# One level of Strassen's algorithm in the second stage of six batches of a fused attention and bilinear kernel

## The chip, the cores and the metric

The kernel runs on one core of one Trainium2 chip. TensorE (PE, with its weight loads shown as PEld), VectorE (DVE), ScalarE (ACT) and GpSimd (POOL) each run their own queue of instructions; SyncE (SP) issues most of the DMAs, and ScalarE's queue issues the stores of the output. The metric is the device time of one execution in microseconds (us): the median of 3 runs. A profile is one further execution; its span runs from the first to the last instruction.

## What is computed

```python
# x: (8, 8, 512, 64) = B, H, S, D     state: (8, 8, 32, 64)
scores  = x @ state^T / sqrt(D);   a  = softmax(scores);   xread = a @ state
scores2 = state @ x^T / sqrt(D);   a2 = softmax(scores2);  sread = a2 @ x
y = concat(xread, sread) over the token axis, heads side by side   # 4608 tokens x 512
h = ((y @ w1) * (y @ w2)) @ w3        # w1, w2: 512 x 1024, w3: 1024 x 1024
out = h @ w_out                       # w_out: 1024 x 512
```

There are 8 batches of 512 token rows (`xread`), and the 32 state rows of each batch (`sread`), which are worked off together at the end, 256 rows in all.

## The kernel before

**What is folded.** `w3 @ w_out` is computed once, into `wo` (1024 x 512), so that the bilinear part needs one product after the elementwise one. `w1` and `w2` are multiplied with each batch's `state` (`sw_steps`, L263, and `per_head`, L140), so that **stage 1** (`stage1`, L297) multiplies `at`, the transposed attention weights (256 values per token: 8 heads of 32 states), by `sw` and gets the two factors directly. Every operand of the large products is split into a high part (ACT casts it to float32r, L96) and a low part (DVE subtracts, L97), by `split` (L93), and a product of two such operands is three matmuls: hi with lo, hi with hi, lo with hi.

**One batch.** The hidden width 1024 is cut into 8 tiles `ft` of 128. For each `ft`, stage 1 runs 12 matmuls of 512 columns (2 factors, 2 tiles of the contraction, 3 parts) into a pair of PSUM banks, `two_banks` (3 such pairs turn). `hidden` (L287) evacuates it, with high priority: ACT copies one factor (L290), DVE multiplies it by the other (L291), ACT and DVE split the result into `g_hi` and `g_lo` (L96, L97), 128 x 512 each. **Stage 2** (`stage2`, L320, with `project`, L313) then takes the 4 token tiles `tt` one after the other: 8 `ft` times 3 matmuls, weights 128 x 128 of `g`, moving operand 128 x 512 of `wo`, all 24 into one bank (`bank`, 2 of these turn), which ACT copies out (L329) and stores from its own queue (L331).

**What runs beside it.** After the first token tile of stage 2 of batch b, `batch_stage2` (L360) runs the steps of `side_steps` (L335): two of the four `sw` units of batch b+1 (16 matmuls of 64 x 32 weights each, then a split of 128 x 1024), the scores of batch b+1 (`scores`, L178, 16 matmuls), the read of batch b (`read_state`, L233, 64 small matmuls with `a2_t` as weights), the other two `sw` units, and the rest of the softmax on DVE and ACT: transposes, maxima, exponentials, sums, and the split into `at_hi` and `at_lo` (L186 to L222). The transposed `e2` is moved block by block with DMAs on SP's queue into `a2_t` (`move_blocks`, L166; L225 to L231), and the read's result into `sread` (L254). At the end of stage 2 come the loads of x (`load_tokens`, `load_x`).

**What sets the order.** PE's and SP's instructions run in the order in which the program lists them (L64). Those of DVE and ACT are put in order when the kernel is built: of what can run, what the program lists first goes first, and what stands under `tc.high_priority()` ahead of the rest. Every engine then works its list strictly from the front. Batch 0 (L462 to L488) has its own, interleaved order and is not changed; batch 1 is the first in the plain loop (L520). The last part, `state_rows` (L492), waits for the last splits of batch 7 (`last_split`, L525), multiplies the 256 state rows with splits of `w1` and `w2` (`grp_z`, L504; L507 and L508) and runs stage 2 on them.

**Buffers that matter here.** `tmp` (4 of 128 x 512) serves the factor copies, and the output tiles; `g_hi` and `g_lo` have 8 buffers each; `work` 2; `x_d` and `x_s` 1 each.

Of the kernel before, what the change touches and what calls it, by code (L numbers as in the profile page):

```python
# [22 lines left out]
F32 = mybir.dt.float32  # L23
# [10 lines left out]
LAST = 5  # L34
PARTS = {0: (640, 1024), 1: (512, 1024)}
WARM = 15

@with_exitstack
def attn_bilinear_kernel(
# [134 lines left out]
    def attention_steps(b):  # L174
        xd = x_tiles[b]
        a2 = {}

        def scores():  # L178

            ps = two_banks()  # L180
            per_head(ps, b, lambda rows, j: xd[rows, j])
            yield
            flat = lambda t: t.rearrange("p k s -> p (k s)")

            s1 = work_tile()
# [37 lines left out]
            yield  # L223

            blocks = work_tile()  # L225
            with tc.issue_after(last[1].ins):
                nc.vector.transpose(out=flat(blocks), in_=flat(e2))
            a2["t"] = work_tile() if b < 2 else late.tile([P, KT, S], F32, name="a2_t")
            tiles = lambda t: t.rearrange("p k (t m) -> p (k t) m", m=P)
            move_blocks(lambda its, j: tiles(a2["t"])[its, :, j * NS:(j + 1) * NS],  # L230
                        lambda mine, c: tiles(blocks)[mine, :, c * NS:(c + 1) * NS])  # L231

        def read_state():  # L233

            xs = token_tiles[b]

            ps = (bank() if b else two_banks()[:, 0])[:, :KT * D].rearrange("p (k d) -> p k d", k=KT)
            for kt in range(KT):
                for t in range(NT):
                    for j in range(NP):  # L240
                        mine = slice(j * NS, (j + 1) * NS)
                        nc.tensor.matmul(  # L242
                            ps[mine, kt], a2["t"][:, kt, t * P + j * NS:t * P + (j + 1) * NS],
                            xs[:, t, 2 * j + kt], start=(t == 0), stop=(t == NT - 1),
                        )
# [45 lines left out]
            nc.vector.tensor_tensor(out=a_sb[:, :n], in0=a_sb[:, :n], in1=ps[:, 1, :n], op=ALU.mult)  # L291
            last_split[:] = split(g_hi, g_lo, a_sb[:, :n])

    def new_g():
        return [main.tile([P, NF], F32R, name=f"g_{part}", bufs=FT) for part in ("hi", "lo")]

    def stage1(b, ft, gs):  # L297
        half, c = divmod(ft * P, NF)
        ps = two_banks()
        hi, lo = at_tiles[b]  # L300
        for i in range(2):
            w_hi, w_lo = sw_tiles[b][half, i]
            k = 0
            for kt in range(KT):
                for w, a in ((w_hi, lo), (w_hi, hi), (w_lo, hi)):
                    nc.tensor.matmul(  # L306
                        ps[:, i], w[:, kt, c:c + P], a[:, kt], start=(k == 0), stop=(k == 3 * KT - 1)
                    )
                    k += 1
        gs.append(new_g())  # L310
        hidden(ps, S, *gs[-1])

    def project(ps, gs, tt, ft):  # L313
# [21 lines left out]
    def side_steps(b):  # L335


        if b == B:
            return [[reads[b - 1]], [], [], []]
        scores, reads[b], a2 = attention_steps(b)  # L340
        w = sw_steps(b)
        softmax = scores()
        first = partial(islice, softmax, 3)
        if b == 1:
            def rest():

# [6 lines left out]
        return [[w[0], w[1], product, reads[b - 1], w[2], w[3], lambda: softmax], [], [], []]  # L353

    def run(steps):
        for step in steps:
# [14 lines left out]
    with tc.tile_pool(name="pro", bufs=2) as pro:  # L371
# [115 lines left out]
        load_tokens(1)  # L487
        load_x(2)  # L488
    late = ctx.enter_context(tc.tile_pool(name="late", bufs=1))


    def state_rows():  # L492
        n = B * NS

        sr = late.tile([P, NP, 2, n], F32R, name="grp_sr")
        split(sr[:, :, 1], sr[:, :, 0], sread)
        gs = []
        for ft in range(FT):
            quarter, c = divmod(ft * P, NQ)
            ps = two_banks()  # L500
            for i in range(2):
                wh, wl = (late.tile([P, NP * P], F32R, name=f"grp_z{q}", bufs=3) for q in range(2))
                as_w = lambda t: t.rearrange("p (j f) -> p j f", j=NP)
                split(as_w(wh), as_w(wl), w_sb[:, quarter, i, :, c:c + P])  # L504
                for kt in range(NP):
                    ks = slice(kt * P, (kt + 1) * P)
                    nc.tensor.matmul(ps[:, i], wh[:, ks], sr[:, kt], start=(kt == 0), stop=False)  # L507
                    nc.tensor.matmul(ps[:, i, :n], wl[:, ks], sr[:, kt, 1], start=False, stop=(kt == NP - 1))  # L508
            gs.append([g[:, :n] for g in new_g()])
            sums = main.tile([P, 2, n], F32, name="tmp", bufs=4)  # L510
            halves = ps.rearrange("p i (half n) -> p i half n", n=n)
            nc.scalar.copy(out=sums, in_=halves[:, :, 1])
            nc.vector.tensor_tensor(out=sums, in0=sums, in1=halves[:, :, 0], op=ALU.add)
            nc.vector.tensor_tensor(out=sums[:, 0], in0=sums[:, 0], in1=sums[:, 1], op=ALU.mult)
            split(*gs[-1], sums[:, 0])
        for tt in range(n // P):
            stage2(gs, tt, [(out[tt * PER + q, S:], q * NS, NS) for q in range(PER)])


    for b in range(1, B):  # L520
        gs = []
        for ft in range(FT):
            stage1(b, ft, gs)
        batch_stage2(b, gs)
    with tc.issue_after(last_split[0].ins), tc.issue_after(last_split[1].ins):  # L525
        state_rows()

# [43 lines left out]
```

## Time and profile before

| | |
|---|---|
| median of 3 runs | 501.19 us (500.25 to 501.69) |
| span of the profiled execution | 498.4 us, at a granted TensorE clock of 0.999 |
| what lies around the span | 1.9 to 3.3 us, if the profiled execution took as long as one of the three runs |
| PE, PEld, DVE, ACT busy | 492.3, 362.8, 285.7, 219.3 us |
| HBM read, written | 38.27 MB, 8.91 MB |

Matmuls are pipelined, so the recorded time of one (about 390 ns for 512 columns) is longer than the distance between two; the distance is read from a chain or a timeline. Weight loads have records of their own (188 ns for 128 x 128), which overlap matmuls. From batch 1 on, the chain of waits repeats the same six pieces of PE work in every batch, some 49 us from one batch to the next; these are shown below.

### The profile page before, as it was taken

Reading aid. Unit: us, or ns where it says so; the run is one execution under the profiler, and the core shown is the slowest. Engines: PE = TensorE matmul, PEld = TensorE weight load, DVE = VectorE, ACT = ScalarE, POOL = GpSimd, SP = SyncE. Lnnn points to the kernel's source line nnn. Section 1 sums busy time; section 2 is a strip of 40 time slices with the busy share of each in tenths; the row PEclk is TensorE's granted clock in tenths of the full one; section 3 lists DMA queues with packets and bytes.
Section 4 is the critical chain, followed back from the end, with each engine's and each line's share of the span. In section 5 each row is a group of like instructions: output and inputs, shape, how many; then the busy total and the mean of one; then the engine's idle time right before and its main releaser. Section 6 shows DMA issues by size and latency. Waiting matters only on the chain.

```text
span 498.4 us, 7562 instructions
## 1 busy us (share of the span) xinstructions
PE 492.3 (99%) x3054; PEld 362.8 (73%) x3054; DVE 285.7 (57%) x394; ACT 219.3 (44%) x325; POOL 0.2 (0%) x4
## 2 busy tenths in 40 slices
PE   8999999999999999999999999999999999999996
PEld 6444467767867886788678867886788678888885
DVE  5669896772539343934393539354934493530780
ACT  4777884443444244334333434243424342431650
POOL 0000000000000000000000000000000000000000
PEclk9999999999999999999999999999999999999999
DMA  8996962013400350035003500350035003301001
GB/s 343 364 380 237 364 264 33 11 47 80 181 22 19 79 189 23 20 79 188 21 27 76 185 22 27 77 184 22 26 78 183 22 26 78 93 24 49 21 1 42
DMA packets 52323, 52.41 MB, mean 105 GB/s; under 512 B 42304, under 2 KB 43328, under 8 KB 47680
## 3 DMA queue, kind: packets, MB, share of 16 engines
q1 hardware_dynamic: 47488, 43.27, 26.3%
q10 hardware_dynamic: 4800, 8.65, 4.6%
q8 instruction: 24, 0.39, 0.3%
q14 instruction: 11, 0.09, 0.1%
HBM read 38.27 MB, written 8.91 MB: 95 GB/s over the span
## 4 chain that ended last, share of the span: by engine, by line
PE 95%; DVE 2%; ACT 2%; DMA 1%; issue 0%; DVEq 0%
PE ps_o L316 38%; PE ps L306 35%; PE ps L146 7%; PE ps L507 3%; PE ps_o L402 3%; PE ps_o L389 3%; PE ps L389 3%; PE ps L508 2%; PE ps_o L242 1%; DMA raw<-in_w_k_dram 1%; ACT ulps L125 0%; ACT w_sb L117 0%; ACT wo_hi L96 0%; DVE w L133 0%; DVE work L204 0%; DVE wo_lo L97 0%
## 5 line engine op out<-in xcount | busy, mean ns | idle before, releaser
L316 PE MATMUL ps_o<-wo_lo,g_hi 128*128 128x512 f32 x272 | 107.0, 394 | 0.0
L316 PE MATMUL ps_o<-wo_hi,g_hi 128*128 128x512 f32 x272 | 106.0, 390 | 0.0
L316 PE MATMUL ps_o<-wo_hi,g_lo 128*128 128x512 f32 x272 | 105.9, 389 | 0.0
L306 PE MATMUL ps<-at_lo,sw_hi 128*128 128x512 f32 x256 | 100.1, 391 | 0.0
L306 PE MATMUL ps<-at_hi,sw_lo 128*128 128x512 f32 x256 | 99.6, 389 | 0.0
L306 PE MATMUL ps<-at_hi,sw_hi 128*128 128x512 f32 x256 | 99.6, 389 | 0.0
L291 DVE TENSOR_TENSOR tmp<-tmp,ps 128x512 f32<-128x512 f32 x64 | 43.9, 687 | 77.0 <-ACT tmp L290 76.9
L97 DVE TENSOR_TENSOR g_lo<-tmp,g_hi 128x512 fp32r<-128x512 f32 (+1 forms) x72 | 47.5, 661 | 41.7 <-ACT g_hi L96 41.6
L96 ACT CAST g_hi<-tmp 128x512 fp32r<-128x512 f32 (+1 forms) x72 | 43.1, 599 | 53.6 <-DVE tmp L291 48.8
L290 ACT COPY tmp<-ps 128x512 f32<-128x512 f32 x64 | 37.7, 589 | 62.8 <-PE ps L306 52.2
L316 PEld LDWEIGHTS ps_o<-wo_lo,g_hi 128*128 128x128 f32 x272 | 51.0, 188 | 18.0 <-issue 7.5
L316 PEld LDWEIGHTS ps_o<-wo_hi,g_lo 128*128 128x128 f32 x272 | 51.1, 188 | 10.8
L316 PEld LDWEIGHTS ps_o<-wo_hi,g_hi 128*128 128x128 f32 x272 | 51.1, 188 | 10.3
L97 DVE TENSOR_TENSOR sw_lo<-ps,sw_hi 128x1024 fp32r<-128x1024 f32 (+1 forms) x34 | 38.4, 1155 | 32.8 <-ACT sw_hi L96 32.8
L306 PEld LDWEIGHTS ps<-at_lo,sw_hi 128*128 128x128 f32 x256 | 48.1, 188 | 10.9 <-issue 1.1
L306 PEld LDWEIGHTS ps<-at_hi,sw_hi 128*128 128x128 f32 x256 | 48.1, 188 | 10.2 <-issue 0.2
L306 PEld LDWEIGHTS ps<-at_hi,sw_lo 128*128 128x128 f32 x256 | 48.1, 188 | 10.0
L329 ACT COPY tmp<-ps_o 128x512 f32<-128x512 f32 x34 | 19.8, 583 | 76.1 <-PE ps_o L316 76.1
L96 ACT CAST sw_hi<-ps 128x1024 fp32r<-128x1024 f32 (+1 forms) x34 | 31.7, 967 | 14.3 <-PE ps L146 14.2
L146 PE MATMUL ps<-w_sb,st 64*32 64x512 f32 (+1 forms) x544 | 31.6, 572 | 0.0
L402 PE MATMUL ps_o<-w_sb,w 128*128 128x512 f32 x64 | 28.5, 599 | 0.1
L402 PEld LDWEIGHTS ps_o<-w_sb,w 128*128 128x128 f32 x64 | 11.8, 190 | 15.9 <-issue 13.8
(65 smaller groups left out, 417.9 us busy)
## 6 DMA issues: line engine op xcount, KB each, us to landing
raw<-in_w_k_dram SPq DMA_DIRECT2D x8, 1024.0 KB, 6.6
x_d<-in_x_d_dram SPq DMA_DIRECT2D x8, 1024.0 KB, 7.1
raw<-in_w_dram SPq DMA_DIRECT2D x8, 1024.0 KB, 6.3
x_s<-in_x_s_dram SPq DMA_DIRECT2D x8, 1024.0 KB, 5.4
out_dram<-tmp ACTq DMA_DIRECT2D x32, 256.0 KB, 2.0
raw<-in_w3t_dram SPq DMA_DIRECT2D x4, 1024.0 KB, 7.2
a_t<-work SPq DMA_DIRECT2D x96, 32.0 KB, 1.9
sread<-turned SPq DMA_DIRECT2D x128, 4.0 KB, 1.7
```

The lines of the kernel that those rows point to most:

```text
L96: nc.scalar.copy(out=hi, in_=src),
L97: nc.vector.tensor_tensor(out=lo, in0=src, in1=hi.bitcast(F32), op=ALU.subtract),
L146: nc.tensor.matmul(ps[j * NS:(j + 1) * NS, q], sts[b][rows, j], moving(rows, j), start=True, stop=True)
L290: nc.scalar.copy(out=a_sb[:, :n], in_=ps[:, 0, :n])
L291: nc.vector.tensor_tensor(out=a_sb[:, :n], in0=a_sb[:, :n], in1=ps[:, 1, :n], op=ALU.mult)
L306: nc.tensor.matmul(ps[:, i], w[:, kt, c:c + P], a[:, kt], start=(k == 0), stop=(k == 3 * KT - 1))
L316: nc.tensor.matmul(ps[:, :DO], g, wo[w][:, ft, :], start=(ft == 0 and k == 0), stop=(ft == FT - 1 and k == 2))
L329: stored[:] = [nc.scalar.copy(out=o, in_=ps[:, :DO])]
L389: nc.tensor.matmul(w34_ps[i][:, :DO], chunks[k][:, DO + i * P:DO + (i + 1) * P], w_out[k], start=(k == 0), stop=(k == FT - 1),)
L402: nc.tensor.matmul(w34_ps[i][:, :DO], w3s[i][:, k * P:(k + 1) * P], w_out[k], start=(k == 0), stop=(k == FT - 1))
L507: nc.tensor.matmul(ps[:, i], wh[:, ks], sr[:, kt], start=(kt == 0), stop=False)
L508: nc.tensor.matmul(ps[:, i, :n], wl[:, ks], sr[:, kt, 1], start=False, stop=(kt == NP - 1))
```

## The change

Batches 0 and 1 keep the old stage 2 (`PLAIN = 2`). For batches 2 to 7 stage 2 is one matrix product, G (512 tokens x 1024) by W (1024 x 512), and both are cut into 2 x 2 blocks: G11 (tokens 0 to 255, `ft` 0 to 3), G12 (`ft` 4 to 7), G21, G22 (tokens 256 to 511), and W likewise. Seven products of a 256 x 512 by a 512 x 256 block (Winograd's form) replace eight. With S1 = G21 + G22, S2 = S1 - G11, S3 = G11 - G21, S4 = G12 - S2, and four combinations `t` of W's blocks made once, the products are G11 W11, G12 W21, S3 T3, G22 T4, S2 T2, S1 T1, S4 W22.

- `combine_weights` (4 calls in batch 1's stage 1) makes the combinations of W's blocks: per call 2 additions of 128 x 512, 4 subtractions of 128 x 256, one split of 128 x 1024.
- `hidden_quarters` replaces `hidden`. `ft` 0 to 3: one factor copy, one multiplication of 128 x 512 into `g_x`, and on every second `ft` a split of G11's two tiles, a subtraction for S3 and its split (128 x 512 each). `ft` 4 to 7: one copy, two multiplications of 128 x 256, a split of 128 x 256 for G12, and on every second `ft` two operations of 128 x 512 for S1 and S2.
- `product` is 24 matmuls with 128 x 128 weights and 256 moving columns. `stage2_quarters` runs seven of them, in the order G11, S3, (side work), G12, G22, S2, S1, S4, and between them the splits of G22, S2, S1 and S4 (two of 128 x 512 each), four operations for S4, three copies of banks on ACT, five sums of 128 x 512 on DVE, and eight stores of 128 x 256 instead of four of 128 x 512.
- In `fast_batch` the read of batch b and the scores of batch b+1 stand after `ft` 3 of stage 1, with the loads of x behind them; two further pieces of the softmax stand after `ft` 4 and `ft` 6; the four `sw` units and the rest of the softmax (`side`) stand after the second product.
- `a2_t` shares `e2`'s one buffer; `g_hi` and `g_lo` have 6 buffers each, which the 14 halves of the seven operands of a batch go through in turn; `state_rows` takes the `x_d` and `sw` buffers.

```diff
-            a2["t"] = work_tile() if b < 2 else late.tile([P, KT, S], F32, name="a2_t")
+            a2["t"] = work_tile() if b < PLAIN else att.tile([P, KT, S], F32, name="e2", bufs=1)
...
+    def combine_weights(k):
+        raw = [tmp_tile() for _ in range(2)]
+        for i, whole in enumerate(raw):
+            nc.vector.tensor_tensor(
+                out=whole, in0=wo["hi"][:, i * QF + k].bitcast(F32), in1=wo["lo"][:, i * QF + k].bitcast(F32), op=ALU.add
+            )
+        b11, b12, b21, b22 = (whole[:, half * HO:(half + 1) * HO] for whole in raw for half in range(2))
+        t = late.tile([P, QF, HO], F32, name="r22")
+        for j, (x, y) in enumerate(((b12, b11), (b22, t[:, 0]), (b22, b12), (b21, t[:, 1]))):
+            nc.vector.tensor_tensor(out=t[:, j], in0=x, in1=y, op=ALU.subtract)
+        split(t_parts["hi"][:, :, k], t_parts["lo"][:, :, k], t)
...
+    def hidden_quarters(ps, ft, q):
...
+        with tc.high_priority():
+            nc.scalar.copy(out=a_sb, in_=ps[:, 0])
+            if ft < QF:
...
+                nc.vector.tensor_tensor(out=q["raw"][p][:, kk], in0=a_sb, in1=ps[:, 1], op=ALU.mult)
+            else:
...
+                nc.vector.tensor_tensor(out=a_sb[:, first], in0=a_sb[:, first], in1=ps[:, 1, first], op=ALU.mult)
+                nc.vector.tensor_tensor(out=q["r22"][:, ft - QF], in0=a_sb[:, second], in1=ps[:, 1, second], op=ALU.mult)
...
+        if ft >= QF:
+            split(*(t[:, kk] for t in q["a12"][p - 2]), a_sb[:, first])
+            if kk:
+                i = p - 2
+                raw, r22 = q["raw"][i], q["r22"][:, 2 * i:2 * i + 2]
+                nc.vector.tensor_tensor(out=raw[:, :, second], in0=raw[:, :, second], in1=r22, op=ALU.add)
+                nc.vector.tensor_tensor(out=raw[:, :, first], in0=raw[:, :, second], in1=raw[:, :, first], op=ALU.subtract)
+        elif kk:
+            raw = q["raw"][p]
+            split(*q["a11"][p], raw[:, :, first])
+            s3 = by_two(tmp_tile())
+            nc.vector.tensor_tensor(out=s3, in0=raw[:, :, first], in1=raw[:, :, second], op=ALU.subtract)
+            split(*q["s3"][p], s3)
+
+    def product(ps, a, w, fresh):
+        for k in range(QF):
+            hi, lo = (t[:, k % 2] for t in a[k // 2])
+            for n, (g, part) in enumerate(((hi, "lo"), (hi, "hi"), (lo, "hi"))):
+                for tt in range(2):
+                    nc.tensor.matmul(
+                        ps[:, tt * HO:(tt + 1) * HO], g[:, tt * P:(tt + 1) * P], w(part, k),
+                        start=(fresh and k == 0 and n == 0 and tt == 0), stop=(k == QF - 1 and n == 2),
+                        skip_group_check=True,
+                    )
+
+    def stage2_quarters(b, q, side):
...
+        bank_a = bank()
+        product(bank_a, q["a11"], b_part(0, 0), True)
+        nc.scalar.copy(out=m1, in_=bank_a)
+        bank_e = bank()
+        product(bank_e, q["s3"], t_part(2), True)
+        nc.scalar.copy(out=m7, in_=bank_e)
+        a22 = quarter_pairs()
+        for i in range(2):
+            split(*a22[i], q["r22"][:, 2 * i:2 * i + 2])
+        side()
+        product(bank_a, q["a12"], b_part(1, 0), False)
+        nc.scalar.copy(out=c11, in_=bank_a)
+        stored_quarter(c11, 0, 0)
+        s2 = quarter_pairs()
...
+            split(*s2[i], s[i])
+        product(bank_e, a22, t_part(3), False)
...
+            nc.vector.tensor_tensor(out=s[i], in0=hi, in1=s[i], op=ALU.subtract)
+            nc.vector.tensor_tensor(out=s[i], in0=lo, in1=s[i], op=ALU.add)
+        s1 = quarter_pairs()
+        for i in range(2):
+            split(*s1[i], q["raw"][i][:, :, HT:S])
+        pair = two_banks()
+        product(pair[:, 0], s2, t_part(1), True)
+        sum2(m1, m1, pair[:, 0])
+        sum2(c21, m1, bank_e)
+        stored_quarter(c21, 1, 0)
...
+            last_split[:] = split(*s4[i], s[i])
+        product(pair[:, 1], s1, t_part(0), True)
+        sum2(m1, m1, pair[:, 1])
+        sum2(m7, m7, m1)
+        stored_quarter(m7, 1, 1)
+        bank_f = bank()
+        product(bank_f, s4, b_part(1, 1), True)
+        sum2(m1, m1, bank_f)
+        stored_quarter(m1, 0, 1)
+
+    def fast_batch(b):
...
+        for ft in range(FT):
+            hidden_quarters(stage1_sums(b, ft), ft, q)
+            if ft == QF - 1:
+                reads[b]()
+                if b + 1 < B:
+                    scores, reads[b + 1], _ = attention_steps(b + 1)
+                    softmax = scores()
+                    next(softmax)
+                    load_tokens(b + 1)
+                if b + 2 < B:
+                    load_x(b + 2)
+            elif ft in (QF, QF + 2):
+                next(softmax, None)
+
+        def side():
+            if b + 1 < B:
+                run(sw_steps(b + 1)[:2])
+                run([lambda: softmax])
+                run(sw_steps(b + 1)[2:])
...
-    for b in range(1, B):
+    for b in range(1, PLAIN):
...
+            if ft % 2:
+                combine_weights(ft // 2)
         batch_stage2(b, gs)
+    for b in range(PLAIN, B):
+        fast_batch(b)
```

More of the change, by code (lines that the diff above doesn't have):

```diff
@@ L36 @@
 WARM = 15
+PLAIN = 2
 @with_exitstack
@@ L292, in hidden, with new_g, stage1_sums @@
             last_split[:] = split(g_hi, g_lo, a_sb[:, :n])
-    def new_g():
-        return [main.tile([P, NF], F32R, name=f"g_{part}", bufs=FT) for part in ("hi", "lo")]
-    def stage1(b, ft, gs):
+    def new_g(ft):
+        if ft < FT - 2:
+            return [main.tile([P, NF], F32R, name=f"g_{part}", bufs=FT - 2) for part in ("hi", "lo")]
+        both = main.tile([P, 2, NF], F32R, name="g_x", bufs=2)
+        return [both[:, 0], both[:, 1]]
+    def stage1_sums(b, ft):
         half, c = divmod(ft * P, NF)
@@ L309, in stage1 @@
                     k += 1
-        gs.append(new_g())
+        return ps
+    def stage1(b, ft, gs):
+        ps = stage1_sums(b, ft)
+        gs.append(new_g(ft))
         hidden(ps, S, *gs[-1])
@@ L353, in side_steps @@
         return [[w[0], w[1], product, reads[b - 1], w[2], w[3], lambda: softmax], [], [], []]
+    QF = FT // 2
+    HT, HO = S // 2, DO // 2
+    def combine_weights(k):
[9 more added lines that the diff above has]
+        split(t_parts["hi"][:, :, k], t_parts["lo"][:, :, k], t)
@@ new lines, in tmp_tile, with quarter_pairs, by_two @@
+    def tmp_tile():
+        return main.tile([P, NF], F32, name="tmp", bufs=4)
+    def quarter_pairs():
+        return [[main.tile([P, 2, HT], F32R, name=f"g_{part}", bufs=FT - 2) for part in ("hi", "lo")] for _ in range(2)]
+    def by_two(t):
+        return t.rearrange("p (k n) -> p k n", k=2)
+    def hidden_quarters(ps, ft, q):
+        a_sb = tmp_tile()
+        p, kk = divmod(ft, 2)
+        first, second = slice(0, HT), slice(HT, S)
+        with tc.high_priority():
+            nc.scalar.copy(out=a_sb, in_=ps[:, 0])
+            if ft < QF:
+                if kk == 0:
+                    q["raw"].append(main.tile([P, 2, NF], F32, name="g_x", bufs=2))
+                nc.vector.tensor_tensor(out=q["raw"][p][:, kk], in0=a_sb, in1=ps[:, 1], op=ALU.mult)
+            else:
+                if ft == QF:
+                    q["r22"] = late.tile([P, QF, HT], F32, name="r22")
+                nc.vector.tensor_tensor(out=a_sb[:, first], in0=a_sb[:, first], in1=ps[:, 1, first], op=ALU.mult)
+                nc.vector.tensor_tensor(out=q["r22"][:, ft - QF], in0=a_sb[:, second], in1=ps[:, 1, second], op=ALU.mult)
+        if ft == 0:
+            q["a11"], q["s3"] = quarter_pairs(), quarter_pairs()
+        elif ft == QF:
+            q["a12"] = quarter_pairs()
+        if ft >= QF:
[11 more added lines that the diff above has]
+            split(*q["s3"][p], s3)
@@ new lines, in stage2_quarters, with stored_quarter @@
+    def stage2_quarters(b, q, side):
+        half = lambda o: slice(o * HO, (o + 1) * HO)
+        b_part = lambda i, o: (lambda part, k: wo[part][:, i * QF + k, half(o)])
+        t_part = lambda j: (lambda part, k: t_parts[part][:, j, k])
+        sum2 = lambda out, x, y: nc.vector.tensor_tensor(out=out, in0=x, in1=y, op=ALU.add)
+        c11, c21, m7, m1 = (tmp_tile() for _ in range(4))
+        def stored_quarter(o, rows, cols):
+            for tt in range(2):
+                first = (2 * rows + tt) * P
+                nc.scalar.dma_start(out=out[b, first:first + P, half(cols)], in_=o[:, half(tt)])
+        bank_a = bank()
[12 more added lines that the diff above has]
+        s2 = quarter_pairs()
+        s = [raw[:, :, 0:HT] for raw in q["raw"]]
+        for i in range(2):
+            split(*s2[i], s[i])
+        product(bank_e, a22, t_part(3), False)
+        for i in range(2):
+            hi, lo = (t.bitcast(F32) for t in q["a12"][i])
+            nc.vector.tensor_tensor(out=s[i], in0=hi, in1=s[i], op=ALU.subtract)
+            nc.vector.tensor_tensor(out=s[i], in0=lo, in1=s[i], op=ALU.add)
+        s1 = quarter_pairs()
+        for i in range(2):
+            split(*s1[i], q["raw"][i][:, :, HT:S])
[4 more added lines that the diff above has]
+        stored_quarter(c21, 1, 0)
+        s4 = quarter_pairs()
+        for i in range(2):
+            last_split[:] = split(*s4[i], s[i])
[7 more added lines that the diff above has]
+        stored_quarter(m1, 0, 1)
@@ new lines, in fast_batch @@
+    def fast_batch(b):
+        q = {"raw": []}
+        softmax = iter(())
+        for ft in range(FT):
[16 more added lines that the diff above has]
+                run(sw_steps(b + 1)[2:])
+        stage2_quarters(b, q, side)
@@ L489, in attn_bilinear_kernel @@
     late = ctx.enter_context(tc.tile_pool(name="late", bufs=1))
+    t_parts = {part: late.tile([P, 4, QF, HO], F32R, name=f"t_{part}") for part in ("hi", "lo")}
     def state_rows():
         n = B * NS
-        sr = late.tile([P, NP, 2, n], F32R, name="grp_sr")
+        sr = att.tile([P, NP, 2, n], F32R, name="x_d", bufs=1)
         split(sr[:, :, 1], sr[:, :, 0], sread)
@@ L501, in state_rows @@
             for i in range(2):
-                wh, wl = (late.tile([P, NP * P], F32R, name=f"grp_z{q}", bufs=3) for q in range(2))
+                wh, wl = (main.tile([P, NP * P], F32R, name=f"sw_{part}", bufs=2 * HALF) for part in ("hi", "lo"))
                 as_w = lambda t: t.rearrange("p (j f) -> p j f", j=NP)
@@ L508, in state_rows @@
                     nc.tensor.matmul(ps[:, i, :n], wl[:, ks], sr[:, kt, 1], start=False, stop=(kt == NP - 1))
-            gs.append([g[:, :n] for g in new_g()])
+            gs.append([g[:, :n] for g in new_g(ft)])
             sums = main.tile([P, 2, n], F32, name="tmp", bufs=4)
```

## The prediction

> **What bounds the kernel now.** I read the page first, then the chain of waits in order of time, then busy times by windows.
>
> ```profile
> PE 492.3 (99%) x3054; PEld 362.8 (73%) x3054; DVE 285.7 (57%) x394; ACT 219.3 (44%) x325; POOL 0.2 (0%) x4
> ...
> PE 95%; DVE 2%; ACT 2%; DMA 1%; issue 0%; DVEq 0%
> ```
>
> TensorE ends everything: 95% of the chain. The chain of waits for one batch (columns: start, length, what):
>
> ```profile
> 267.77 21.76 PE ps L306 x96
> 289.53 5.44 PE ps_o L316 x24
> 294.97 2.74 PE ps L146 x48
> 297.71 1.03 PE ps_o L242 x64
> 298.74 1.91 PE ps L146 x32
> 300.65 16.59 PE ps_o L316 x72
> 317.23 21.76 PE ps L306 x96
> ```
>
> Stage 1 is 96 matmuls in 21.76 us, 0.2267 us each, though their records last 0.39. Stage 2's first 24 have the same 0.2267; the other 72 take 16.59 instead of 16.32, so 0.27 is lost on coming out of the side work, which I let stand. A batch is 317.23 - 267.77 = 49.46 us without a hole. So time is won by fewer or shorter matmul slots, and lost where another engine is late. How much room does VectorE leave?
>
> ```profile
> 243.00:267.77 24.77, 24.77 (x229) 17.66 (x228) 16.24 (x20) 8.96 (x13) 0.00 (x0) 1.00 0.12 38
> 267.77:289.53 21.76, 21.76 (x98) 18.02 (x97) 9.60 (x14) 9.07 (x15) 0.00 (x0) 1.00 0.44 133
> ```
>
> The columns after the length are PE, PEld, DVE and ACT busy, POOL, clock, DMA. The first window is the side work: 16.24 us of DVE in 20 operations (softmax, sw splits, the read). In the second, stage 1, DVE is busy 9.60 of 21.76 us, PE in both all the time.
>
> **The change, part by part.** *Matmuls.* Stage 2 has 4 x 24 = 96 slots of 512 columns, 21.76 us. The new one has 7 x 24 = 168 slots of 256 columns, each with its own weights. Equal columns per load would be 84 x 0.2267 = 19.04 us, or 0.113 per slot; what a slot really costs stands in the last part, where 256 columns (L508) alternate with 512 (L507). The timeline there, of PE and then of PEld:
>
> ```profile
> 469.78 0.28 PE L508 MATMUL ps<-grp_sr,grp_z 128*128 128x256 f32 x1
> 469.90 0.40 PE L507 MATMUL ps<-grp_sr,grp_z 128*128 128x512 f32 x1
> 470.14 0.28 PE L508 MATMUL ps<-grp_sr,grp_z 128*128 128x256 f32 x1
> 470.26 0.40 PE L507 MATMUL ps<-grp_sr,grp_z 128*128 128x512 f32 x1
> ...
> 474.38 0.28 PE L508 MATMUL ps<-grp_sr,grp_z 128*128 128x256 f32 x1
> ```
>
> ```profile
> 470.14 0.19 PEld L507 LDWEIGHTS ps<-grp_sr,grp_z 128*128 128x128 f32 x1
> 470.26 0.19 PEld L508 LDWEIGHTS ps<-grp_sr,grp_z 128*128 128x128 f32 x1
> ```
>
> After a 256-column matmul the next begins 0.12 later, with weights whose load began together with that 256-column matmul: the load is ready within 0.12. The 13 pairs from 469.78 to 474.38 take 0.354 each; with 0.2267 for the 512 columns, 0.127 is left for the 256. No row shows 256 columns after 256 columns. Ends: 0.113 and 0.127; I take 0.120, the distance seen. Then a product is 24 x 0.120 = 2.88 us, seven are 20.16, and 1.60 us is won per batch: 6 x 1.60 = **9.6 us** (16.3 at 0.113, 2.5 at 0.127).
>
> The Trainium skill, "TensorE: Matmul & The Clock Gate", section "The mechanism" in Part 3, says that a weight load overlaps running matmuls only when it goes to another row group. All our loads fill all rows, so by it each slot would be load plus matmul. The trace disagrees (the load at 470.14, beside the L508 matmul, and its user at 470.26); that it could still hold for a pure stream is a rival below.
>
> *VectorE's new work.* Durations, from the groups of instructions by form:
>
> ```profile
> L97 DVE TENSOR_TENSOR g_lo<-tmp,g_hi 128x512 fp32r<-128x512 f32 x64 | 44.2, 691 | 40.7 <-ACT g_hi L96 40.6
> L97 DVE TENSOR_TENSOR g_lo<-tmp,g_hi 128x256 fp32r<-128x256 f32 x8 | 3.4, 420 | 0.9 <-ACT g_hi L96 0.9
> L97 DVE TENSOR_TENSOR sw_lo<-ps,sw_hi 128x1024 fp32r<-128x1024 f32 x30 | 35.8, 1218 | 32.8 <-ACT sw_hi L96 32.8
> L96 ACT CAST g_hi<-tmp 128x512 fp32r<-128x512 f32 x64 | 39.8, 623 | 48.8 <-DVE tmp L291 48.8
> L290 ACT COPY tmp<-ps 128x512 f32<-128x512 f32 x64 | 37.7, 589 | 62.8 <-PE ps L306 52.2 <-DMA a_t<-work 10.7
> ```
>
> Before: 16 operations of 0.69 in a batch, 11.0 us. After, in stage 1: 4 multiplications of 0.69, 8 of 0.42, 4 low parts of 0.42, 4 operations of 0.69 for S1 and S2, and 2 x 3 of 0.69 for G11 and S3: 14.7 us. In stage 2: 8 low parts, 4 operations for S4, 5 sums, 17 x 0.69 = 11.7. With the side work's 16.24 that is 42.6 us of DVE in a batch whose PE work is 49.46 - 1.60 = 47.9: 89% against 27.3 of 49.46. It fits, but not where it falls. The tight stretch runs from the end of the scores (after `ft` 3) to the start of product S1, for most of the side work now comes ahead of S1's split in the program.
>
> PE's time in it: 4 groups of stage 1, 4 x 2.72 = 10.88; products G11, S3, G12, G22, S2, 5 x 2.88 = 14.40; the four sw units, 64 of the 80 matmuls that take 2.74 + 1.91 = 4.65, so 3.72. Sum 29.0 us.
>
> DVE's work in it: side work 16.24; what is left of `ft` 3's group: its matmuls end 1.03 + 0.93 = 1.96 earlier (read and scores), the copy takes 0.59 and the multiplication 0.69, so 0.68 remains for 3 x 0.69 = 2.07, 1.39 is left; `ft` 4 to 7: 12 x 0.42 + 4 x 0.69 = 7.80; splits of G22, S2, S1, 6 x 0.69 = 4.14; S4's operations 2.76. Sum 32.3 us, 3.3 too much. But operations that wait for nothing overlap a little. DVE's timeline has three in a row, and, in the side work, one wait:
>
> ```profile
> 262.80 1.23 DVE L97 TENSOR_TENSOR at_lo<-work,at_hi 128x1024 fp32r<-128x1024 f32 x1 [1.11 <-ACT at_hi L96]
> ...
> 440.58 1.89 DVE L97 TENSOR_TENSOR grp_z<-w_sb,grp_z 128x512 fp32r<-128x512 f32 x3
> ```
>
> Three of 0.69 in 1.89: they start 0.60 apart, 0.09 saved each. For 25 of the 29 new operations (two S1/S2 pairs and two S4 pairs, where each second one needs the first, get nothing) that is 2.2: 30.1 us, **1.1 us late per batch**. S1's product can begin on half its operand, 0.69 earlier; I set that against waits of DVE for ACT's casts, of which the side work shows the one of 1.11 behind its first split. The bounds: 0 (the last transposition, L227, 1.2 us, may be put later) and 3.3 + 1.1 = 4.4 (nothing overlaps, one such wait). After S1 the pressure ends: 18.6 us of PE to the next scores against some 10 of DVE. The lag comes up in batches 2 to 6; batch 7 has no side work. 5 x 1.1 = **5.5 us**.
>
> The Trainium skill, "VectorE: DVE Perf Modes", section "The DRAIN you can't avoid", has the next operation wait until the pipeline is empty, and adds that one that isn't held starts earlier. The first half alone would make it 32.3 us and 5 x 3.3 = 16.5; the row of three is on the side of the second.
>
> *ACT.* Stage 1: 8 copies of 0.59, 8 casts of at most 0.62; stage 2: 8 casts, 3 copies; the side work's window 8.96: at most 25.4 of 47.9 us. The queue stands still where a store waits for a DVE sum: a cast for S4 behind the store of the third quarter would come late. I cost it at nothing, for S4's casts can run before the sum is there; if they stand behind, it is part of the 4.4.
>
> *combine_weights*, batch 1 only: 4 x (2 x 0.69 + 4 x 0.42 + 1.22) = 17.1 us of DVE. Three calls, 12.8, fall in batch 1's stage 1, where DVE is idle some 12.2 (the window row above is of a like batch); the pairs of banks let PE run two groups, 5.4 us, ahead. Cost 0; 0.6 if that cover is gone.
>
> *What is moved.* Read and scores are the same PE slots elsewhere. SP's queue now has the read's 16 block moves, then the loads of x, behind `ft` 3, and the moves of `a2_t` some 25 us later:
>
> ```profile
> 267.88 7.81 SPq L170 DMA_DIRECT2D a_t<-work  x12
> 276.05 0.33 SPq L158 DMA_DIRECT2D x_s<-in_x_s_dram  x1
> 276.90 0.42 SPq L154 DMA_DIRECT2D x_d<-in_x_d_dram  x1
> ```
>
> 0.65 us each: 16 take 10.4, done before `a2_t`'s moves start; `a2_t` is then read some 20 us after its transposition, x a batch after its load. Cost 0. Eight stores of 128 KB for four of 256 KB wait for nothing on PE's path. *The end:* `state_rows` may start after S4's split of batch 7, a product or two (3 to 6 us) before stage 2 ends; its first splits, of 1024 and of 512 columns, take DVE 1.22 + 0.69 and ACT about as much, under 4 us. Cost 0, at worst 2.
>
> **The sum.** -9.6 + 5.5 = -4.1 us. The profiled span of 498.4 becomes 494.3; the median, 2.8 above it (what lies around the span and the scatter of 500.25 to 501.69), becomes 501.19 - 4.1 = **497.1 us**.
>
> **The rivals.**
> - *No lag*: DVE's order puts late work late. 501.2 - 9.6 = 491.6, at 0.113 per slot 484.9. For it: 89% is below 100%. Against: the 29.0 us sum.
> - *VectorE becomes the bound in that stretch* (slower): operations don't overlap, since most follow a cast of ACT, and PE waits 3.3 us before S1 in five batches: 501.2 - 9.6 + 16.5 = 508.1, with the one wait for ACT 513.6. It cancels the gain from 9.6 / 5 = 1.9 us per batch. For it: every g_lo of today waits for ACT (40.6 us idle in 64). Against: beside the side work's other operations DVE runs 20 of them with one such wait behind the first split.
> - *Slots of 0.127*: gain 2.5, lag 5.5: 504.2; without lag 498.7.
> - *The load isn't hidden in a pure stream*: 0.12 + 0.12 per slot, 40.3 us in place of 21.76: 6 x 18.6 = 111 us more, about 612. The pairs above speak against it.
>
> **How the numbers follow.** Forecast 42%, its own range 493 to 501; no lag 19%; VectorE bound 26%; slots of 0.127 10%; load not hidden 3%. Leaving out the last, the upper third of the VectorE case and the fastest end of "no lag" gives 487 to 511. 0.3% (1.5 us) is about what a measurement of this kernel can tell from no change. Faster by more (under 499.7): three quarters of the forecast, nearly all of "no lag", a fifth of the 0.127 case: 0.53. Within it: 0.14. Slower: 0.33.
>
> **What would show it.** Starts 0.12 apart for the new matmuls, 2.88 us per product in the chain; a DVE entry of about 1 us ahead of S1 in batches 2 to 6 and none in batch 7; DVE near 85 to 90% busy from batch 2 on; no DMA in the chain after batch 1. Wrong would make it: a slot apart from 0.113 to 0.127, PE waiting ahead of `sw` or stage 1, or a DVE order in which casts and low parts alternate without other work between.

## The result, and the profile after

| | before | after |
|---|---|---|
| median | 500.73 us (500.25 to 501.69, 4 runs) | 522.79 us (522.62 to 523.51, 4 runs) |
| ratio after to before | | 1.0441 (95% interval 1.0425 to 1.0457) |
| span of the profiled execution | 498.4 us | 521.0 us |
| mean granted TensorE clock | 0.999 | 0.990 |

The changed kernel is 4.4% slower, outside the range given (487 to 511). The page of after, busy times and the chain by engine:

```profile
PE 492.1 (94%) x3486; PEld 379.7 (73%) x3486; DVE 376.6 (72%) x584; ACT 239.5 (46%) x371; POOL 0.2 (0%) x4
...
PE 69%; DVE 21%; ACT 5%; issue 4%; DMA 1%; DVEq 0%; ACTq 0%
```

TensorE's busy time is what it was (492.3 before), but its share fell from 99% to 94%: about 29 us without a matmul, where there were 6. VectorE rose from 285.7 to 376.6 us and holds 21% of the chain. What TensorE waited for, from the view of waits (who, for whom: us in total, times, the longest):

```profile
PE ps L147 <- DVE sw_lo L98: 11.8, 6, 2.3
PE ps L427 <- DVE tmp L437: 5.5, 6, 1.1
PE ps_o L243 <- issue: 4.1, 1, 4.1
```

Three waits, 21.4 us. The first is a `sw` unit, the fourth in batches 2 to 6 and, for 1.2 us, the third in batch 1; the second a product of `stage2_quarters`, in batches 2 to 7; the third the read of batch 2, once. The chain of batch 5, in parts (start, length, what):

```profile
333.48 10.92 PE ps L310 x48
...
368.75 1.09 PE ps L147 x16
369.85 5.95 PE ps_o L427 x48
375.80 2.89 PE ps L427 x24
378.71 0.70 DVE tmp L437
379.54 3.11 PE ps L427 x24
382.65 2.88 PE ps_o L427 x24
385.54 10.92 PE ps L310 x48
```

A product that isn't entered out of a wait takes 2.88 us for 24 matmuls, 0.120 each, as forecast. So 1.60 us of slots were won in each batch, and the batch still became 52.06 us long (49.46 before). From the starts of stage 1 in the two chains:

| batch | 1 | 2 | 3 | 4 | 5 | 6 | 7 and the end |
|---|---|---|---|---|---|---|---|
| before, us | 49.44 | 49.46 | 49.42 | 49.46 | 49.43 | 49.46 | 82.28 |
| after, us | 50.96 | 57.13 | 53.53 | 52.04 | 52.06 | 53.52 | 81.94 |
| difference | +1.52 | +7.67 | +4.11 | +2.58 | +2.63 | +4.06 | -0.34 |

With the 0.37 by which batch 1 starts later this is the 22.6 us between the spans. Four things are in it.

**The fourth sw unit.** The timeline of batch 5, VectorE, then ScalarE, then TensorE:

```profile
364.57 1.25 DVE L98 TENSOR_TENSOR g_lo<-g_x,g_hi 128x512 fp32r<-128x512 f32 x2
365.74 0.69 DVE L465 TENSOR_TENSOR g_x<-g_hi,g_x 128x512 f32<-128x512 f32 x1
366.34 1.22 DVE L98 TENSOR_TENSOR at_lo<-work,at_hi 128x1024 fp32r<-128x1024 f32 x1
367.48 1.22 DVE L98 TENSOR_TENSOR sw_lo<-ps,sw_hi 128x1024 fp32r<-128x1024 f32 x1
```

```profile
364.69 1.05 ACT L97 CAST at_hi<-work 128x1024 fp32r<-128x1024 f32 x1
365.64 2.83 ACT L97 CAST sw_hi<-ps 128x1024 fp32r<-128x1024 f32 x3
```

```profile
363.69 2.81 PE L147 MATMUL ps<-w_sb,st 64*32 64x512 f32 x48
368.75 1.09 PE L147 MATMUL ps<-w_sb,st 64*32 64x512 f32 x16 [2.25 <-DVE sw_lo L98]
```

Three units fill the three pairs of banks from 363.69 on. The fourth needs the first pair back, and that pair's split (`sw_lo`, 367.48) stands on VectorE behind S2's two low parts, S4's first operation and `at_lo`, and its cast on ScalarE behind `at_hi`. Before the change the scores and the read stood between the units.

**A product behind a sum.** S1's product (379.54) begins right behind the sum `tmp` L437 (378.71), which adds S2's product to M1. Nothing of S1 needs that sum. But the two products are written to the two banks of one `pair`.

**Batch 2's read.** SP's queue, and the chain:

```profile
177.82 1.92 SPq L171 DMA_DIRECT2D e<-work  x3
179.84 0.54 SPq L159 DMA_DIRECT2D x_s<-in_x_s_dram  x1
180.90 0.43 SPq L155 DMA_DIRECT2D x_d<-in_x_d_dram  x1
```

```profile
181.66 4.08 issue
185.74 2.48 PE ps_o L243 x64
188.34 1.64 PE ps L147 x16
```

The read is ready to go at 181.66, but its tokens (`x_s`) were only asked for at 179.84, behind the block moves of batch 1's side work, and arrive 5.7 us later. The profile calls such a wait "issue".

**The clock.** The read takes 2.48 us instead of 1.03, the scores 1.64 instead of some 0.9. By windows (length; PE, PEld, DVE, ACT and POOL busy; clock; DMA):

```profile
185.70:190.00 4.30, 4.13 (x81) 2.44 (x81) 1.11 (x3) 0.00 (x0) 0.00 (x0) 0.60 0.36 152
...
263.20:265.70 2.50, 2.50 (x24) 1.66 (x25) 2.50 (x3) 1.02 (x1) 0.00 (x0) 0.79 0.01 3
265.70:268.20 2.50, 2.50 (x15) 2.50 (x14) 2.50 (x4) 0.62 (x1) 0.00 (x0) 0.53 0.31 50
...
316.70:319.20 2.50, 2.49 (x28) 1.66 (x29) 2.50 (x3) 1.02 (x1) 0.00 (x0) 1.00 0.01 1
```

Behind the wait of 4.08 us the granted clock is 0.60. Behind the wait ahead of the fourth sw unit (1.56 us in batch 2, 2.23 to 2.27 in batches 3 to 6) it falls to 0.53 in batch 3 (third row) and stays at 1.00 in batch 4 (last row); products G12 and G22 together then take 7.43 and 7.32 us in batches 3 and 6, where they take 5.95 in the others.

Why two pauses out of five? In shorter windows the clock goes from 1.00 to 0.50 at 186.12, 264.63 and 421.64 us, and stays there for 3.41 us each time. These falls (a fourth follows the last matmul) are 78.51 and 157.01 us apart, 23 and 46 times 3.413 us, so they lie on one grid. Counted by the steps of this grid, TensorE was idle for 3.03, 1.95 and 2.23 of the 3.41 us ahead of the three falls. The pauses of batches 2, 4 and 5 are cut by a border of the grid, which leaves at most 1.12, 1.39 and 1.72 us of idle time in one step, and the clock stays. So a pause of 2.2 us is charged or not by where it falls.

The Trainium skill, "TensorE: Matmul & The Clock Gate", section "What's actually happening", has the clock halved after an idle window of about 3.4 us, and calls the window free-running. The grid agrees with a window that runs freely; that 1.95 us of idle time in it are enough is less than the page gives.

### The profile page after: what moved, and what is told of

It is laid out like the page before. It is cut to its first block, busy times and chain, and to the rows that moved or that the text cites. A ratio compares the mean times of both kernels' runs of the same rounds, so it can differ in the third digit from the quotient of the medians.

```text
span 521.0 us, 8784 instructions
## 1 busy us (share of the span) xinstructions
PE 492.1 (94%) x3486; PEld 379.7 (73%) x3486; DVE 376.6 (72%) x584; ACT 239.5 (46%) x371; POOL 0.2 (0%) x4
## 4 chain that ended last, share of the span: by engine, by line
PE 69%; DVE 21%; ACT 5%; issue 4%; DMA 1%; DVEq 0%; ACTq 0%
PE ps L310 24%; PE ps_o L427 12%; PE ps_o L324 10%; PE ps L427 6%; PE ps L147 3%; DVE g_lo L98 3%; PE ps L665 3%; PE ps_o L559 3%; PE ps_o L546 3%; PE ps L546 3%; PE ps L666 1%; DVE sw_lo L98 1%; ACT e L197 1%; DVE at_lo L98 1%; DVE work L187 1%
## 5 line engine op out<-in xcount | busy, mean ns | idle before, releaser
L397 DVE TENSOR_TENSOR g_x<-tmp,ps 128x512 f32<-128x512 f32 x24 | 16.5, 687 | 44.1 <-ACT tmp L393 44.1
L147 PE MATMUL ps<-w_sb,st 64*32 64x512 f32 (+1 forms) x544 | 31.8, 572 | 11.8 <-DVE sw_lo L98 11.8
L97 ACT CAST g_hi<-g_x 128x512 fp32r<-128x512 f32 x48 | 29.5, 620 | 27.8 <-PE ps_o L427 13.9
L97 ACT CAST g_hi<-tmp 128x256 fp32r<-128x256 f32 (+1 forms) x54 | 27.1, 502 | 31.7 <-DVE tmp L401 16.3
L98 DVE TENSOR_TENSOR g_lo<-g_x,g_hi 128x512 fp32r<-128x512 f32 x48 | 31.9, 686 | 3.1 <-ACT g_hi L97 2.0
L98 DVE TENSOR_TENSOR g_lo<-tmp,g_hi 128x256 fp32r<-128x256 f32 (+1 forms) x54 | 29.1, 540 | 4.2 <-ACT g_hi L97 3.6
L427 PE MATMUL ps_o<-wo_lo,g_hi 128*128 128x256 f32 x144 | 30.7, 296 | 0.0
L427 PE MATMUL ps_o<-wo_hi,g_lo 128*128 128x256 f32 x144 | 30.1, 292 | 0.0
L427 PE MATMUL ps_o<-wo_hi,g_hi 128*128 128x256 f32 x144 | 30.0, 291 | 0.0
L147 PEld LDWEIGHTS ps<-w_sb,st 64*32 64x32 f32 x544 | 8.2, 106 | 28.7 <-DVE sw_lo L98 17.4
L427 PEld LDWEIGHTS ps_o<-wo_lo,g_hi 128*128 128x128 f32 x144 | 24.1, 202 | 4.8 <-issue 3.5
L427 PE MATMUL ps<-t_lo,g_hi 128*128 128x256 f32 x96 | 19.8, 288 | 5.5 <-DVE tmp L437 5.5
```

The source lines that it names most:

```text
L97: nc.scalar.copy(out=hi, in_=src),
L98: nc.vector.tensor_tensor(out=lo, in0=src, in1=hi.bitcast(F32), op=ALU.subtract),
L147: nc.tensor.matmul(ps[j * NS:(j + 1) * NS, q], sts[b][rows, j], moving(rows, j), start=True, stop=True)
L397: nc.vector.tensor_tensor(out=q["raw"][p][:, kk], in0=a_sb, in1=ps[:, 1], op=ALU.mult)
L427: nc.tensor.matmul(ps[:, tt * HO:(tt + 1) * HO], g[:, tt * P:(tt + 1) * P], w(part, k), start=(fresh and k == 0 and n == 0 and tt == 0), s ...
```

## The experiments

The theory I started from (A): three waits, each with a cause of its own, and the clock behind them. The rival (B): VectorE is full from the scores to S1's split (busy for 31.77 of the 32 us from 345 to 377), and whatever wait is taken away comes back at the next operand. All runs are measured against the kernel before on the same chip.

**e1_pair: a pair of banks for each of S2 and S1.**

```diff
-        pair = two_banks()
-        product(pair[:, 0], s2, t_part(1), True)
-        sum2(m1, m1, pair[:, 0])
+        for_s2, for_s1 = two_banks()[:, 0], two_banks()[:, 0]
+        product(for_s2, s2, t_part(1), True)
+        sum2(m1, m1, for_s2)
...
-        product(pair[:, 1], s1, t_part(0), True)
-        sum2(m1, m1, pair[:, 1])
+        product(for_s1, s1, t_part(0), True)
+        sum2(m1, m1, for_s1)
```

> Products S2 and S1 get a pair of PSUM banks each, where they shared one. Theory A (three waits, each with its own cause): the first matmul of S1 stands behind the sum that reads the bank of S2 only because both banks are one tile; the entry wait of 0.87 us and the slow restart of 0.2 go in six batches, 6 x 1.1 = 6.6 us, to about 516. Theory B (VectorE is full from the scores to S1's split, and any wait that is removed comes back at the next operand): S1's operand is what is late, the wait stays, 521 to 523.

513.34 us (ratio 1.0259, 1.0225 to 1.0293), 9.5 below after. The entry of L437 is gone from TensorE's waits, a plain batch is 50.94 us, 1.1 shorter, and the two products run as one piece (its chain, batch 4):

```profile
314.05 5.94 PE ps_o L427 x48
319.99 5.76 PE ps L427 x48
325.75 2.88 PE ps_o L427 x24
328.63 10.92 PE ps L310 x48
```

So S1's operand was not late: A. Of the rest some is clock, which here fell behind one wait for a sw unit, not behind two.

**e2_sw3: the fourth sw unit behind product G12.**

```diff
-                run(sw_steps(b + 1)[2:])
+                run(sw_steps(b + 1)[2:3])
...
         stored_quarter(c11, 0, 0)
+        if b + 1 < B:
+            run(sw_steps(b + 1)[3:])
```

> The fourth sw unit of the next batch stands behind product G12 and no longer ahead of it. Theory A: it waits for a pair of PSUM banks that VectorE frees late, and G12 needs nothing of it; 2.25 us of idle PE go in batches 2 to 6, 11.3 us, and with them the falls of the clock in batches 3 and 6, 2.9 us: about 509. Theory B: VectorE has the same work to do before S1 and S4, so PE waits there instead: 520 to 523, with a new entry of about 2 us ahead of S1 or S4.

514.98 us (1.029, 1.0265 to 1.0315), 7.8 below after: between the two. Its waits:

```profile
PE ps L427 <- DVE tmp L437: 10.3, 6, 1.9
PE ps_o L243 <- issue: 3.1, 1, 3.1
...
PE ps L147 <- DVE sw_lo L98: 1.2, 1, 1.2
```

The sw unit waits no longer (but in batch 1), and S1 waits longer, 1.9 us instead of 0.9, for the same sum. TensorE comes to S1 sooner, while VectorE is still at the splits of S1, of the fourth sw unit and of S4, behind which the sum stands. That half came back looks like B, but the sum isn't needed there; the fourth run tells.

**e3_tokens: batch 2's tokens ahead of batch 1's block moves.**

```diff
-        return [[w[0], w[1], product, reads[b - 1], w[2], w[3], lambda: softmax], [], [], []]
+        return [[w[0], w[1], product, reads[b - 1], w[2], w[3], lambda: load_tokens(b), lambda: softmax], [], [], []]
...
-        if b + 1 < B:
-            load_tokens(b + 1)
```

> Batch 2's tokens are loaded ahead of the 16 block moves of batch 1's side work on SP's queue, and no longer behind them. Theory A: the read of batch 2, which the change puts 20 us earlier, waits 4.08 us for that load, and the clock that falls in the wait costs 2.2 us more: about 516.5, with no entry of the read in PE's waits. Theory B: batch 2's second half of stage 1 then waits for VectorE as the other batches do, and 1 to 3 us of the 6.3 come back: 518 to 520.

519.72 us (1.0374, 1.0348 to 1.04), 3.1 below after, half of the 6.3 and in B's range. The read no longer waits; instead an entry of 2.5 us stands ahead of the scores of batch 2, for which the profile names a DVE split. Their x (`x_d`) is the load next in SP's queue.

**e6_move_alone: eight products, but read and scores in the middle of stage 1.** In `fast_batch`, with the old `stage1` and `stage2`, and without the combinations of W:

```diff
+        for tt in range(NT):
+            stage2(gs, tt, [(out[b, tt * P:(tt + 1) * P], 0, P)])
+            if tt == 0 and b + 1 < B:
+                run(sw_steps(b + 1)[:2])
+                run([lambda: softmax])
+                run(sw_steps(b + 1)[2:])
```

> The plain stage 2 of eight products in all batches, without the combinations of W, but read and scores in the middle of stage 1 and the softmax pieces where the change has them. Theory A: the move brings only the wait of batch 2 for its tokens, 4.1 and 2.2 us for the clock: 507. A rival, the move costs VectorE's order in every batch (1 to 2 us each): 512 to 518. If the move is free: 501.

513.34 us (1.0246, 1.0229 to 1.0263): the move alone costs 12.7 us, in the lower part of the rival's range. Batch 2 has its loads; and every other batch is 50.56 us instead of 49.46, with a wait of 0.7 us for the first unit's split in each (3.6 in 5). VectorE is no busier than before there, 26.95 us a batch (27.29 before): the wait comes from the cover that was moved away. Beside the crowded VectorE of after it is 2.25.

**e4_three: e1, e2 and e3 together.**

> The three edits of the runs before together: own pairs for S2 and S1, the fourth sw unit behind G12, batch 2's tokens ahead of the block moves. Apart they gave 9.4, 7.8 and 3.1 us, 20.3 in all. Theory A (separate waits): 502.5 if they only add up; since what was left of the wait ahead of S1 in the second run is the same sum that the first run takes out of the way, another 4 to 5 us: 498 to 502, a plain batch at 49 us. Theory B (VectorE full): the batch stays near 50.9 us, 505 to 508, with a new wait for a split.

502.09 us (1.0022, 1.0006 to 1.0038), 20.7 below after, where the three apart gave 20.3. The entries of L427 and, but for batch 1, of L147 for sw are gone: with its own banks S1 does not care about the late sum. B would have left a wait for a split in batches 2 to 7, and there is none above 0.2 us; the 2.8 us ahead of batch 2's scores are still there.

**e5_undo_move: seven products, read and scores back in stage 2** (the read ahead of the first product, the scores behind the second sw unit).

```diff
-                run([lambda: softmax])
+                scores, reads[b + 1], _ = attention_steps(b + 1)
+                softmax = scores()
+                next(softmax)
                 run(sw_steps(b + 1)[2:])
+                run([lambda: softmax])
...
+        reads[b]()
         stage2_quarters(b, q, side)
```

> Seven products as in the change, but read and scores back in stage 2 (the read ahead of the first product, the scores behind the second sw unit, all of the softmax behind them). Theory A: the waits for batch 2's tokens go (6 us), S1's wait for the sum stays, and the third sw unit now waits for its banks behind a VectorE that has all of the softmax in stage 2: 516 to 522. A rival, that the move itself is the larger part of the loss (alone it measured 12.7 us): 508 to 512.

528.42 us (1.0561, 1.0542 to 1.058), worse than after and than both expectations. S1's product waits 16.6 us in 6 for the sum, up to 3.8, and the sw units 9.6 in 6. With all of the softmax and some eleven more microseconds of VectorE work in stage 2, the sum and the sw splits come late. So in this form the seven products are better off with the move. Whether they would be with a pair of banks each for S2 and S1 is not shown: this run keeps the shared pair, through which the larger of its two waits goes.

**e7_loads: e4_three with batch 3's x, too, ahead of the moves.**

```diff
-..., w[3], lambda: load_tokens(b), lambda: softmax], [], [], []]
+..., w[3], lambda: load_tokens(b), lambda: load_x(b + 1), lambda: softmax], [], [], []]
```

> As e4_three, and batch 3's x too is loaded ahead of the block moves, for the scores that the change puts into batch 2. Theory A: the wait of 2.5 us ahead of the scores in e3_tokens was for this load and not for VectorE, whose name the profile gives; 2.5 us and some of the clock go: 2 to 4 us below e4_three. Theory B: it was for VectorE, and the time is that of e4_three within 1 us.

499.58 us (0.9983, 0.997 to 0.9995), 2.5 below e4_three: the scores had waited for the load, whatever name stood there. Now the read of batch 2 waits 2.1 us for the block moves into `a2_t`, which end later, behind the loads.

**e8_pool: e7_loads with the sums of combine_weights on GpSimd** (`nc.gpsimd` for `nc.vector` in its six operations).

> As e7_loads, with the additions and subtractions of combine_weights on GpSimd instead of VectorE, in batch 1 alone. Batch 1 became 1.5 us longer by the change, in which PE waits for VectorE; if that is combine_weights' share of VectorE, 1 to 2 us below e7_loads. If it is the turning of the tmp buffers, which it still holds, no gain, or a loss where GpSimd takes longer: up to 3 us above.

503.35 us (1.007, 1.0046 to 1.0095), 3.8 above e7_loads, more than either expectation. One addition of 128 x 512 takes GpSimd 1.66 us (VectorE 0.69), and ScalarE's casts of the combinations, with the casts for `g` in line behind them, wait for it. The group on GpSimd, and ScalarE's wait from batch 1:

```profile
L370 POOL TENSOR_TENSOR tmp<-wo_hi,wo_lo 128x512 f32<-128x512 f32 x8 | 13.2, 1661 | 122.8 <-DMA out_dram<-tmp 122.6
```

```profile
ACT t_hi L97 <- POOL r L376: 5.8, 4, 1.7
```

**e9b_loads and e9_best.** Both: e1 and e2, batch 3's x right behind the scores of batch 2, the tokens ahead of the moves. e9_best also spreads combine_weights over batch 1.

```diff
+        return [[w[0], w[1], product, lambda: load_x(b + 1), reads[b - 1], w[2], w[3], lambda: load_tokens(b), lambda: softmax], [], [], []]
...
-            if ft % 2:
-                combine_weights(ft // 2)
+            if ft in (3, 7):
+                combine_weights(ft // 4)
...
             run(side[tt])
+            if tt in (1, 2):
+                combine_weights(tt + 1)
```

> As e9_best, but with combine_weights where the change has it: tells the two edits apart. Theory A: 1 to 2 us above e9_best, 496 to 498; if the loads alone do it, the same as e9_best; if the combinations alone do it, e7_loads' 499.6.

> As e7_loads, with batch 3's x loaded right behind the scores of batch 2, ahead of the read's moves too, and with combine_weights called at tiles 3 and 7 of batch 1's stage 1 and after the second and third token tile of its stage 2. Theory A (each wait has its own cause): the 2.1 us that batch 2's read still waits for the moves of a2_t go, for the moves no longer stand behind a load of 8 us, and batch 1 is back near its 49.4 us: 494 to 497. A rival, VectorE in batch 1 has too much to do wherever the combinations stand: 498 to 500.

e9b_loads: 497.71 us (0.9939, 0.9926 to 0.9953), 1.9 below e7_loads, with no wait above 0.2 us left in batch 2. e9_best: **496.01 us (0.9905, 0.989 to 0.9919)**, another 1.7, and 0.95% below the kernel before. Both edits count, as A had it. One batch of e9_best, then one of after, by windows:

```profile
267.34:316.14 48.80, 48.60 (x410) 40.26 (x409) 39.67 (x63) 21.77 (x37) 0.00 (x0) 1.00 0.26 79
```

```profile
333.48:385.54 52.06, 48.73 (x410) 40.24 (x409) 39.66 (x63) 22.10 (x37) 0.00 (x0) 1.00 0.24 74
```

The same matmuls, the same 39.7 us of VectorE, and 3.26 us less time: VectorE was not the bound of after; two orders were.

**e10_move_mended: eight products, the move, with the loads and the sw unit in order.**

> Eight products and the moved read and scores, as in e6_move_alone, with the two edits of the loads and the fourth sw unit one token tile later; no combinations of W. Theory A: the move costs only by the loads (6 to 7 us of its 12.7) and by the wait of the fourth sw unit, for which read and scores were the cover (0.7 us of idle and a slow restart in each batch): 501 to 503. A rival, the move costs in another way, by more entries into the large matmuls: 504 to 508.

503.67 us (1.0059, 1.0044 to 1.0075), between the two expectations. No wait above 0.2 us is left from batch 1 on, and still the batch is 50.02 us, 0.56 more than before. The chain of one batch, in parts:

```profile
319.44 10.88 PE ps L310 x48
330.32 1.03 PE ps_o L243 x64
331.35 1.02 PE ps L147 x16
332.37 11.11 PE ps L310 x48
343.47 5.44 PE ps_o L324 x24
348.91 2.73 PE ps L147 x48
351.64 5.67 PE ps_o L324 x24
357.32 1.02 PE ps L147 x16
358.33 11.12 PE ps_o L324 x48
```

48 large matmuls take 10.88 us behind large ones, 11.11 behind the scores; 24 take 5.44 and 5.67. Each entry from small weights into large ones costs 0.23 us, each of the one-unit pieces another 0.1. Before there was one such entry per batch (the 0.27 that the prediction let stand), now there are three.

## Why the prediction was wrong, step by step

- **The slot of 0.120 us: right.** Products take 2.88 us. The 0.127 and the 0.113 were not needed, and a pure stream of 256 columns hides its loads too: the rule of the Trainium skill that the prediction weighed ("TensorE: Matmul & The Clock Gate", "The mechanism", which elsewhere in that section also lets a load into the background weight buffer go ahead) does not hold here.
- **VectorE's work: right in size.** 42.6 us by durations, measured 39.7, for operations with nothing to wait for overlap, 0.07 us for each of the 43 new ones (0.09 taken for 25). The lag "1.1 us late per batch" ahead of S1 was the failed reading of it. TensorE did wait 0.9 us there, in batches 2 to 7, batch 7 too, which has no side work: that was the sum in the same pair of banks (e1_pair). With this and the sw unit mended no wait ahead of S1 is left (e4_three), so S1's operand was not late enough to cost anything. Forecast and measurement, 5.5 us both, agree here by luck: the number is the same and the cause is not.
- **"Read and scores are the same PE slots elsewhere", cost 0: the step that failed most.** They were the work that hid the return of the first pair of banks to the fourth sw unit. Without it TensorE waits 0.7 us a batch beside an easy VectorE (e6_move_alone), 1.56 to 2.27 beside a crowded one, 10.6 us in batches 2 to 6. I counted the slots and didn't ask what they covered. The entries into the large matmuls, three for one, are another 0.56 us a batch (e10_move_mended).
- **"x a batch after its load", cost 0: wrong for the first of the changed batches.** Batch 1 still loads at its end, batch 2 already reads in the middle of stage 1: 4.08 us and the clock behind it for the tokens, and 2.5 us for the x of the scores once these are mended (e3_tokens, e7_loads).
- **The clock was not in the sum.** In a kernel without a hole it has no place; with holes it took some 2.2 us in batch 2 and 1.4 in each of batches 3 and 6.
- **combine_weights, cost 0 to 0.6:** 1.5 us, 1.7 by e9_best against e9b_loads. VectorE had room for it in stage 1 on paper; it pushed the sw splits behind it, and a unit waited 1.2 us in batch 1 too.
- **The rivals.** "VectorE becomes the bound" had the sign and the stretch, but not the mechanism: it foresaw waits for operands, and with 39.7 us in the 48.80 of e9_best it is refuted as the bound. What is true of it is that a crowded VectorE made each badly placed wait longer. It also reached only to 513.6, so the measured 522.8 lay beyond every rival but the load that isn't hidden. Of the prediction's own signs of being wrong, TensorE waiting ahead of `sw` came true. "No lag", 491.6, is what e9_best comes near, at 496.0; the difference is 0.9 us a batch of entries and small waits in five batches.
- **The sum that holds:** for after, in the profiled execution: -9.6 for the slots, +10.6 for the fourth sw unit, +6.9 ahead of S1 (5.5 of wait and six entries of 0.23), +4.1 for the tokens, +5.0 for the clock, +1.5 for the combinations, +0.4 for the later start of batch 1, and, as an estimate from e10_move_mended, 5 x 0.56 = +2.8 for entries. That is 21.7 of the 22.6 us. For the mended kernel: move mended +3.0 (500.65 to 503.67), seven products for eight -7.7 (to 496.01): five batches of 50.02 - 48.80 = 1.22, one of 1.6. The 26.8 us between e9_best and after are the two waits, the loads, the combinations, and the clock behind them.

Not settled: how much of the clock's fall belongs to which wait, since executions of the same order differ (e3_tokens from 517.42 to 520.72 us); how much idle time in one step of the grid is enough, since in e1_pair 1.81 us were not and in e2_sw3 1.86 were, but falls also followed 1.63 us in e6_move_alone and 1.13 in e8_pool; and the rule by which a pair's two banks are held together was shown only by giving each product its own pair.

## What to carry to other kernels

When a step is moved in an in-order queue, ask what it covered where it stood (here the turning of three pairs of banks) and what had been started early enough for it only because it was late (here the loads of the first changed batch). A saving of 3% of the slots of a full engine is smaller than two waits of 1 to 2 us in each batch, so mend those first: in the view of waits, the entries that occur once per batch are the price list. Products that don't depend on each other shouldn't share one tile's banks when something reads the first while the second is due.

## What the hardware showed that I had not expected

- TensorE's granted clock fell to 0.50 for 3.41 us at a time, on a grid of 3.413 us. In after, 1.95 us of idle time within one step of the grid were enough and 1.72 were not, so of four pauses of 2.2 us two cost clock and two did not.
- Coming from small weights into 128 x 128 weights costs 0.23 us per entry, 11.11 for 10.88 and 5.67 for 5.44, with no wait in the profile.
- Loads of 128 x 128 weights are hidden behind matmuls of 256 columns for all of a product: 24 in 2.88 us, though each load is recorded with 0.19 us and the distance is 0.12.
